# Single-pass matrix products whose moving operand is read as two interleaved halves: a spectral and attention mix on one core

## The chip, the cores and the metric

The kernel runs on one NeuronCore of one Trainium2 chip. The metric is the device time of one execution in microseconds. Three runs of the kernel before gave 1774.73, 1778.48 and 1774.53; their median is 1774.73.

TensorE (PE in the profile) multiplies: a weight load (PEld) puts the stationary operand into the array, and a matmul streams the moving operand's columns past it and adds into a bank of PSUM. VectorE (DVE), ScalarE (ACT) and GpSimd (POOL) work element by element, and SyncE (SP) starts most of the DMA transfers.

## What is computed

```python
a = jnp.einsum("bsd,ed->bse", x, dft_hid_re)
b = jnp.einsum("bsd,ed->bse", x, dft_hid_im)
y = jnp.einsum("ts,bse->bte", dft_seq_re, a) - jnp.einsum("ts,bse->bte", dft_seq_im, b)
...
q = (lambda x, *d: x.transpose(*d))((x @ wq).reshape(B, S, H, Dh), 0, 2, 1, 3)
k = x @ wk
v = x @ wv
scores = jnp.einsum("bhqd,bkd->bhqk", q, k) * (Dh ** -0.5)
p = _softmax(scores, axis=-1)
o = jnp.einsum("bhqk,bkd->bhqd", p, v)
return (lambda x, *d: x.transpose(*d))(o, 0, 2, 1, 3).reshape(B, S, H * Dh) @ wo
...
g = _sigmoid((x * gate_w).sum(-1, keepdims=True))
return g * a + (1 - g) * b
```

The sizes are S = 2048, D = 640, 32 heads of 20 with one key and one value head for all of them, everything in float32. In the last line a is the spectral branch's y and b is the attention branch.

## The kernel before, in words

**Number formats.** A value is split in two parts of the format float32r, a high part (the value rounded, made by a copy) and a low part (the value minus the high part). A product is then two or three matmuls of float32r operands: high by high, high by low, low by high. Both formats have four bytes to an element. A float32r matmul streams its columns once; the text calls it a single-pass product. One product, the attention weights by the values (`av`), has plain float32 operands instead, and its matmul streams the columns in two passes, as its time shows.

**Stages.** The work goes through five stages, each with its own products.

1. From 7 us: q and kv. `q_mm` (through `mm3`, L112) and `kv_mm` (L207) multiply x^T, split, by the weights; the moving operand is 512 columns of x^T. `q_out` and `kv_out` split the results and send them to DRAM and to the key tile `ks`. In the same stage the two hidden DFT matrices are loaded in ten pieces (`load_w`) and split (`split_w`).
2. From 89 us: `ab`, x by the hidden DFT matrices (`mm3_rows`, L120). The contraction of 128 rows is cut into two halves of 64 rows. Each half has its own rows of the array and its own bank, and the two run side by side. The moving operand is 320 columns of the split DFT matrix. Among these products stand the first 160 `a` units.
3. From 250 us to 1579 us: the main stage, in which four kinds of product are mixed. `a` (`a_unit`) is queries by keys, with 512 key columns moving; DVE reads each result of 128 x 512 and reduces it to a row maximum. `b` (`b_unit`) is keys by queries, with 512 query columns moving; ACT reads each result and takes the exponential into a tile `pt`. `av` (`av_mm`) multiplies `vsb` by four `pt` tiles of 512 columns, in four column groups of the array side by side. `y` (`Halves.run`) is the sequence DFT matrix by the results of `ab`, with 320 columns moving, 64 rows at a time; seven products replace eight. `a`, `b` and `y` each use one half of the array's rows, so that a product of one kind can run in the upper half beside another in the lower half. `av` uses all rows.
4. From 1579 us to 1702 us: the rest of `b`, `av` and `y`.
5. To the end: `o` (`o_group`, through `mm3`), the attention result by `wo`, with 320 columns of the split `wo` moving. `load_wo` splits `wo` in stage 4.

**What sets the order.** All engines but SP follow the order in which the code issues the instructions. In the main stage this order is the string PLAN: `V` is four `av` products, `0` and `1` are a `y` product in the lower or upper half of the rows, and a letter is an `a` or `b` unit with its half and one of six PSUM banks, which `a` and `b` share. A unit that takes a bank waits until DVE or ACT has read that bank's previous result.

Of the kernel before, what the change touches and what calls it, by code (L numbers as in the profile page):

```python
# [8 lines left out]
F32 = mybir.dt.float32  # L9
# [25 lines left out]
def kernel(  # L35
# [63 lines left out]

    nc.scalar.activation(gate, ident[:, :NT], AF.Exp)  # L100

    def words(ap):
        return ap.bitcast(F32) if ap.dtype == F32R else ap

# [6 lines left out]

    def mm3(ps, wh, wl, xh, xl, n, i):  # L112

        nc.tensor.matmul(ps, wh, xh, start=(i == 0), stop=False)  # L114
        nc.tensor.matmul(ps, wh, xl, start=False, stop=False)  # L115
        nc.tensor.matmul(ps, wl, xh, start=False, stop=(i == n - 1))  # L116

# [2 lines left out]
    def mm3_rows(ps2, wh, wl, xh, xl, n, i):  # L122
        for k, (w, x) in enumerate(((wh, xh), (wh, xl), (wl, xh))):
            for ps, r in zip(ps2, RG):
                nc.tensor.matmul(  # L125
                    ps, w[r], x[r], start=(i == 0 and k == 0), stop=(i == n - 1 and k == 2)
                )

    xT_v = xT.rearrange("(c p) t -> p c t", p=P)
# [13 lines left out]
    def split_w(i, c):  # L143
        if i < 2:
            if c == 0:
                wh.append(w2.tile([P, KC, D], F32R, name=f"wh{i}"))
                wl.append(w2.tile([P, KC, D], F32R, name=f"wl{i}"))
            split(wraw.pop((i, c)), wh[i][:, c], wl[i][:, c])

    xraw, xspl = {}, {}  # L150

# [13 lines left out]
    with ExitStack() as c1:  # L165
# [33 lines left out]
        def q_out(ps, n, m):  # L199
            ms, ts = slice(m * P, (m + 1) * P), slice(n * ROW, (n + 1) * ROW)  # L200
            qh = x1.tile([P, ROW], F32R, name="qh", bufs=4)
            ql = x1.tile([P, ROW], F32R, name="ql", bufs=4)
            nc.scalar.activation(qh, ps, AF.Copy)
            nc.vector.tensor_tensor(ql, ps, qh.bitcast(F32), op=ALU.subtract)
            move(qh_d[ms, ts], qh)
            move(ql_d[ms, ts], ql)

        def kv_mm(ps, n, c):
            xh, xl = xsp[n]
            nc.tensor.matmul(ps, kvgs[:, c], xh[:, c], start=(c == 0), stop=False)  # L210
            nc.tensor.matmul(ps, kvgs[:, c], xl[:, c], start=False, stop=(c == KC - 1))  # L211

        def kv_out(ps, n):
            ts = slice(n * ROW, (n + 1) * ROW)
            kvT = x1.tile([41, ROW], F32, name="kvT")
            kh = x1.tile([DH, ROW], F32R, name="kh")
            kl = x1.tile([DH, ROW], F32R, name="kl")
            nc.scalar.activation(kvT, ps[64:105], AF.Copy)
            nc.vector.tensor_tensor(kvT, ps[:41], kvT, op=ALU.add)
            nc.scalar.activation(kh, kvT[:DH], AF.Copy)  # L220
            nc.vector.tensor_tensor(kl, kvT[:DH], kh.bitcast(F32), op=ALU.subtract)
            for r0 in (0, 64):
                move(ks[r0 : r0 + 20, ts], kh)
                move(ks[r0 + 20 : r0 + 40, ts], kl)
                move(ks[r0 + 40 : r0 + 60, ts], kh)
            return kvT
# [95 lines left out]
    def a_unit(u, hh, tag="A"):  # L322

        p, r = divmod(u, 64)
        qb, c = divmod(r, 4)
        if r == 0 and p not in mx:
            mx[p] = sml.tile([P, 2, NT, 4], F32, name="mx")
        b = 64 * hh
        ps = bank(tag, f"a_{u}_{hh}")
        nc.tensor.matmul(  # L330
            ps,
            qs[p][b : b + 60, qb * P : (qb + 1) * P],
            ks[b : b + 60, c * ROW : (c + 1) * ROW],
            start=True,
            stop=True,
        )
        return nc.vector.tensor_reduce(mx[p][:, hh, qb, c : c + 1], ps, axis=AX.X, op=ALU.max)  # L337
# [223 lines left out]
    def load_wo(cs):  # L561
        for c in cs:
            raw = xp.tile([P, D], F32, tag=f"xr{c % 2}", name="woraw")
            move(raw, wo[c * P : (c + 1) * P])
            t = abp.tile([P, 2, D], F32R, tag=f"ab{c}0", name=f"wo{c}")
            split_w = (t[:, 0], t[:, 1])
            nc.vector.tensor_copy(split_w[0], raw)
            nc.vector.tensor_tensor(split_w[1], raw, split_w[0].bitcast(F32), op=ALU.subtract)
            wos[c] = split_w

    oT_v = oT_d.rearrange("(c p) t -> p c t", p=P)
# [64 lines left out]
    class Halves:  # L636
# [11 lines left out]
        def run(self, g):  # L648
# [4 lines left out]
            k = 0 if one else g  # L653
            start, stop = grp[k] == 0, grp[k] == (6 if one else 3) * NT - 1
            grp[k] += 1
            mm = nc.tensor.matmul(ps[g % len(ps)], w, x, start=start, stop=stop)  # L656
            if one:

                if not start and self.last != g:
# [122 lines left out]
    def b_unit(p, hh, kc, qc, tag):  # L782
        b = 64 * hh
        ps = bank(tag, f"b_{p}_{kc}_{qc}_{hh}")
        nc.tensor.matmul(  # L785
            ps,
            ks[b : b + 62, kc * P : (kc + 1) * P],
            qs[p][b : b + 62, qc * ROW : (qc + 1) * ROW],
            start=True,
            stop=True,  # L790
        )
        n = taken["b"][0] + taken["b"][1]
        slot = pick(waits(tag, n))
        t = pp.tile([P, ROW], F32, tag=f"pt{slot}", name="pt")
        halves.scored(nc.scalar.activation(t, ps, AF.Exp, scale=SCALE), n)  # L795
        pt[(hh, kc, qc)] = t, (n, slot)
# [293 lines left out]
```

## Time and profile before

| | |
|---|---|
| median of three runs | 1774.73 us (1774.53 to 1778.48) |
| the profiled execution, first to last instruction | 1773.9 us |
| mean granted TensorE clock | 1.000 |
| busy: PE, PEld, DVE, ACT, POOL | 1766.9, 1263.5, 1425.3, 1187.5, 819.7 us |
| DMA, share of the 16 engines | 42.4% in the largest queue |

The profiled execution is 0.8 us shorter than the median of the runs, so a difference in the profile can be set against the runs as it stands. PE's busy time is a union of pipelined instructions whose ends are modelled: a matmul of 320 columns is shown as 309 ns long, although the next one starts after 147 ns. How fast PE really streams is therefore read from the distance between starts.

### The profile page before, as it was taken

The numbers are of one execution on the slowest core, as the hardware profiler recorded it, in microseconds if no ns is written. First come the engines' busy times: TensorE is split into PE (matmuls) and PEld (weight loads), VectorE is DVE, ScalarE is ACT, GpSimd is POOL, SyncE is SP. The second block draws the span as 40 slices with busy tenths as digits, with TensorE's granted clock in tenths as the row PEclk, the third lists the DMA queues.
The fourth block names the chain that finished last, engine by engine and source line by source line (L and its number), as shares of the span: only waits on it lengthen the run. The fifth ranks groups of instructions, "written<-read, shape, count | busy, mean of one in ns | idle before, by whom it ended". The sixth has DMA issues, their size and how long they took to land.

```text
span 1773.9 us, 40730 instructions
## 1 busy us (share of the span) xinstructions
PE 1766.9 (100%) x16342; PEld 1263.5 (71%) x16342; DVE 1425.3 (80%) x2335; ACT 1187.5 (67%) x2327; POOL 819.7 (46%) x559
## 2 busy tenths in 40 slices
PE   9999999999999999999999999999999999999999
PEld 7799986666666666666666666666666666667789
DVE  4469999888888888888888888888888898855344
ACT  4432247777777777777777777777777777777731
POOL 1001227444455465656666565565654454442242
PEclk9999999999999999999999999999999999999999
DMA  8762324333334442534444444343443232325676
GB/s 268 233 198 95 116 98 133 108 130 100 125 106 146 119 132 92 174 99 159 151 143 123 156 131 132 103 148 106 142 141 113 86 119 89 103 67 188 191 230 206
DMA packets 131001, 243.87 MB, mean 137 GB/s; under 512 B 26356, under 2 KB 77556, under 8 KB 128292
## 3 DMA queue, kind: packets, MB, share of 16 engines
q1 hardware_dynamic: 130012, 238.00, 42.4%
q0 software_dynamic: 800, 3.28, 0.6%
q8 instruction: 128, 2.10, 0.5%
q14 instruction: 61, 0.50, 0.1%
HBM read 194.62 MB, written 50.86 MB: 138 GB/s over the span
## 4 chain that ended last, share of the span: by engine, by line
PE 99%; DMA 0%; ACT 0%; DVE 0%; issue 0%
PE av L799 27%; PE y L656 21%; PE b L785 17%; PE a L330 17%; PE ab L125 8%; PE q L114 1%; PE o L114 1%; PE q L116 1%; PE q L115 1%; PE o L116 1%; PE o L115 1%; PE kv L210 0%; PE kv L211 0%; DMA xr<-in_xT_dram 0%; ACT pt L795 0%; DVE mx L337 0%
## 5 line engine op out<-in xcount | busy, mean ns | idle before, releaser
L337 DVE TENSOR_REDUCE mx<-a 128x1 f32<-128x512 f32 x2048 | 1264.9, 683 | 170.5 <-PE a L330 111.3
L795 ACT ACTIVATE pt<-b 128x512 f32<-128x512 f32 x2048 | 1052.0, 618 | 327.8 <-PE b L785 193.5
L656 PE MATMUL y<-x,ch 64*128 64x320 f32 x3584 | 758.3, 309 | 0.9 <-ACT yt L685 0.9
L330 PE MATMUL a<-ks,qs 60*128 60x512 f32 x2048 | 736.4, 422 | 0.2 <-DVE mx L337 0.2
L785 PE MATMUL b<-qs,ks 62*128 62x512 f32 x2048 | 705.9, 421 | 0.3 <-ACT half L533 0.3
L656 PEld LDWEIGHTS y<-x,ch 64*128 64x128 f32 x3584 | 560.3, 185 | 23.0 <-issue 10.4
L656 PE MATMUL y<-x,cl 64*128 64x320 f32 x1792 | 514.9, 308 | 0.0
L799 PE MATMUL av<-pt,vsb 128*32 128x512 f32 x4096 | 502.9, 600 | 0.0
L330 PEld LDWEIGHTS a<-ks,qs 60*128 60x128 f32 x2048 | 350.1, 184 | 128.1 <-DVE mx L337 98.3
L785 PEld LDWEIGHTS b<-qs,ks 62*128 62x128 f32 x2048 | 340.3, 184 | 129.6 <-ACT pt L795 70.8
L459 POOL TENSOR_TENSOR craw<-craw 128x1024 f32<-128x1024 f32 x80 | 191.2, 2390 | 261.6 <-DMA craw<-in_cre_dram 115.4
L656 PEld LDWEIGHTS y<-x,cl 64*128 64x128 f32 x1792 | 308.4, 184 | 3.9 <-issue 2.5
L799 PEld LDWEIGHTS av<-pt,vsb 128*32 128x32 f32 x4096 | 106.6, 108 | 201.0 <-issue 179.0
L464 POOL TENSOR_TENSOR cl<-craw,ch 128x1024 fp32r<-128x1024 f32 x98 | 234.6, 2394 | 7.8
L463 POOL CAST ch<-craw 128x1024 fp32r<-128x1024 f32 x98 | 101.7, 1038 | 146.8 <-PE y L656 123.4
L125 PE MATMUL ab<-wh,xh 64*128 64x320 f32 x640 | 129.6, 307 | 0.0
L125 PE MATMUL ab<-wl,xh 64*128 64x320 f32 x640 | 129.3, 306 | 0.0
L125 PE MATMUL ab<-wh,xl 64*128 64x320 f32 x640 | 129.1, 305 | 0.0
L712 POOL TENSOR_TENSOR ya<-yt,ya 128x320 f32<-128x320 f32 x64 | 57.9, 920 | 102.5 <-ACT yt L685 101.8
L533 ACT ACTIVATE half<-ab 128x320 f32<-128x320 f32 x64 | 28.0, 438 | 114.8 <-PE ab L125 82.4
L125 PEld LDWEIGHTS ab<-wl,xh 64*128 64x128 f32 x640 | 91.5, 185 | 0.0
L125 PEld LDWEIGHTS ab<-wh,xl 64*128 64x128 f32 x640 | 91.3, 184 | 0.0
(88 smaller groups left out, 1082.7 us busy)
## 6 DMA issues: line engine op xcount, KB each, us to landing
craw<-in_cre_dram SPq DMA_DIRECT2D x96, 512.0 KB
craw<-in_cim_dram SPq DMA_DIRECT2D x96, 512.0 KB
xr<-x_d SPq DMA_DIRECT2D x88, 320.0 KB
qs<-qh_d SPq DMA_DIRECT2D x64, 160.0 KB
x_d<-both SPq DMA_DIRECT2D x64, 160.0 KB
ya<-y_d SPq DMA_DIRECT2D x64, 160.0 KB
y_d<-ya SPq DMA_DIRECT2D x64, 160.0 KB
xr<-in_xT_dram SPq DMA_DIRECT2D x20, 256.0 KB
```

What stands on the lines that cost most here:

```text
L114: nc.tensor.matmul(ps, wh, xh, start=(i == 0), stop=False)
L125: nc.tensor.matmul(ps, w[r], x[r], start=(i == 0 and k == 0), stop=(i == n - 1 and k == 2))
L330: nc.tensor.matmul(ps, qs[p][b : b + 60, qb * P : (qb + 1) * P], ks[b : b + 60, c * ROW : (c + 1) * ROW], start=True, stop=True,)
L337: return nc.vector.tensor_reduce(mx[p][:, hh, qb, c : c + 1], ps, axis=AX.X, op=ALU.max)
L459: eng.tensor_tensor(raw, raw, raws[1], op=PRODUCTS[n][0][1])
L463: eng.tensor_copy(h, raw)
L464: eng.tensor_tensor(l, raw, h.bitcast(F32), op=ALU.subtract)
L656: mm = nc.tensor.matmul(ps[g % len(ps)], w, x, start=start, stop=stop)
L712: nc.gpsimd.tensor_tensor(ya, yt, ya, op=how)
L785: nc.tensor.matmul(ps, ks[b : b + 62, kc * P : (kc + 1) * P], qs[p][b : b + 62, qc * ROW : (qc + 1) * ROW], start=True, stop=True,)
L795: halves.scored(nc.scalar.activation(t, ps, AF.Exp, scale=SCALE), n)
L799: nc.tensor.matmul(ps[32 * g : 32 * g + 32, :], vsb[:, kc, :], t, start=first, stop=last)
```

## The change

Every float32r matmul gets its moving operand through `woven`, which reads column 0, then the first column of the second half, then column 1, and so on: with 512 columns 0, 256, 1, 257, ..., with 320 columns 0, 160, 1, 161, .... The columns of the result stand in the order in which they were read. `av` is left as it was, and the weight loads are too.

So that the output comes out in its natural order, the order is undone where elements are copied anyway: at q's split and the DFT matrix's split by reading every fourth element and writing four runs (two woven products follow one another there), at kv's eviction and `wo`'s split by reading every second element and writing two runs. The splits of the DFT matrices and of `wo` are done in two halves of 320 columns each, since each half of 320 is a moving operand of its own.

```diff
+    def woven(ap):
+        return ap.rearrange("p (a b) -> p b a", a=2)
+    def runs(ap):
+        return ap.rearrange("p (a b) -> p a b", a=4)
+    def every(ap, n=4):
+        return ap.rearrange("p (b a) -> p a b", a=n)
...
     def mm3(ps, wh, wl, xh, xl, n, i):
-        nc.tensor.matmul(ps, wh, xh, start=(i == 0), stop=False)
-        nc.tensor.matmul(ps, wh, xl, start=False, stop=False)
-        nc.tensor.matmul(ps, wl, xh, start=False, stop=(i == n - 1))
+        nc.tensor.matmul(ps, wh, woven(xh), start=(i == 0), stop=False)
+        nc.tensor.matmul(ps, wh, woven(xl), start=False, stop=False)
+        nc.tensor.matmul(ps, wl, woven(xh), start=False, stop=(i == n - 1))
...
-                    ps, w[r], x[r], start=(i == 0 and k == 0), stop=(i == n - 1 and k == 2)
+                    ps, w[r], woven(x[r]), start=(i == 0 and k == 0), stop=(i == n - 1 and k == 2)
...
-            split(wraw.pop((i, c)), wh[i][:, c], wl[i][:, c])
+            raw = wraw.pop((i, c))
+            for e in range(2):
+                es = slice(e * HALF, (e + 1) * HALF)
+                hi, lo = wh[i][:, c, es], wl[i][:, c, es]
+                nc.scalar.activation(runs(hi), every(raw[:, es]), AF.Copy)
+                nc.vector.tensor_tensor(
+                    runs(lo), every(raw[:, es]), runs(hi).bitcast(F32), op=ALU.subtract
+                )
...
-            nc.scalar.activation(qh, ps, AF.Copy)
-            nc.vector.tensor_tensor(ql, ps, qh.bitcast(F32), op=ALU.subtract)
+            nc.scalar.activation(runs(qh), every(ps), AF.Copy)
+            nc.vector.tensor_tensor(runs(ql), every(ps), runs(qh).bitcast(F32), op=ALU.subtract)
...
-            nc.scalar.activation(kvT, ps[64:105], AF.Copy)
-            nc.vector.tensor_tensor(kvT, ps[:41], kvT, op=ALU.add)
+            kvW = kvT.rearrange("p (a b) -> p a b", a=2)
+            nc.scalar.activation(kvW, every(ps[64:105], 2), AF.Copy)
+            nc.vector.tensor_tensor(kvW, every(ps[:41], 2), kvW, op=ALU.add)
...
-            ks[b : b + 60, c * ROW : (c + 1) * ROW],
+            woven(ks[b : b + 60, c * ROW : (c + 1) * ROW]),
...
-            nc.vector.tensor_copy(split_w[0], raw)
-            nc.vector.tensor_tensor(split_w[1], raw, split_w[0].bitcast(F32), op=ALU.subtract)
+            for e in range(2):
+                es = slice(e * HALF, (e + 1) * HALF)
+                hi, lo = [w[:, es].rearrange("p (a b) -> p a b", a=2) for w in split_w]
+                nc.vector.tensor_copy(hi, every(raw[:, es], 2))
+                nc.vector.tensor_tensor(lo, every(raw[:, es], 2), hi.bitcast(F32), op=ALU.subtract)
...
-            mm = nc.tensor.matmul(ps[g % len(ps)], w, x, start=start, stop=stop)
+            mm = nc.tensor.matmul(ps[g % len(ps)], w, woven(x), start=start, stop=stop)
...
-            qs[p][b : b + 62, qc * ROW : (qc + 1) * ROW],
+            woven(qs[p][b : b + 62, qc * ROW : (qc + 1) * ROW]),
```

In `kv_mm` the two matmuls get `woven(xh[:, c])` and `woven(xl[:, c])` in the same way.

The order of the instructions on PE, POOL and SP is the same as before; on ACT and DVE the pieces of the DFT matrix split, and on DVE those of the `wo` split, become two. This is DVE in stage 1, between two results of q (`xl` is the low part of the next x, `ql` that of a q result, `wl` that of a DFT matrix piece), before:

```order
L204 TENSOR_TENSOR ql<-q_0_347,qh 128x512
L110 TENSOR_TENSOR wl_374<-wraw,wh_373 128x640
L110 TENSOR_TENSOR xl<-xr,xh 128x512
L204 TENSOR_TENSOR ql<-q_1_379,qh 128x512
L110 TENSOR_TENSOR wl_374<-wraw,wh_373 128x640
```

and in the changed kernel:

```order
L223 TENSOR_TENSOR ql<-q_0_347,qh 128x512
L165 TENSOR_TENSOR wl_374<-wraw,wh_373 128x320 x2
L122 TENSOR_TENSOR xl<-xr,xh 128x512
L223 TENSOR_TENSOR ql<-q_1_381,qh 128x512
L165 TENSOR_TENSOR wl_374<-wraw,wh_373 128x320 x2
```

Nothing has moved; one instruction of 640 columns is two of 320. On ACT the same piece reads, before:

```order
L203 ACTIVATE qh<-q_0_347 128x512
L109 ACTIVATE wh_373<-wraw 128x640
L109 ACTIVATE xh<-xr 128x512
L203 ACTIVATE qh<-q_1_379 128x512
L109 ACTIVATE wh_373<-wraw 128x640
```

and in the changed kernel:

```order
L222 ACTIVATE qh<-q_0_347 128x512
L164 ACTIVATE wh_373<-wraw 128x320 x2
L121 ACTIVATE xh<-xr 128x512
L222 ACTIVATE qh<-q_1_381 128x512
L164 ACTIVATE wh_373<-wraw 128x320 x2
```

The high part's copy is halved too, at the same place.

More of the change, by code (lines that the diff above doesn't have):

```diff
@@ L209, in kv_mm @@
             xh, xl = xsp[n]
-            nc.tensor.matmul(ps, kvgs[:, c], xh[:, c], start=(c == 0), stop=False)
-            nc.tensor.matmul(ps, kvgs[:, c], xl[:, c], start=False, stop=(c == KC - 1))
+            nc.tensor.matmul(ps, kvgs[:, c], woven(xh[:, c]), start=(c == 0), stop=False)
+            nc.tensor.matmul(ps, kvgs[:, c], woven(xl[:, c]), start=False, stop=(c == KC - 1))
         def kv_out(ps, n):
```

## The prediction

> **What bounds the kernel now.** I read the chain of waits first, then the stages, then the starts of single matmuls.
>
> ```profile
> PE 99%; DMA 0%; ACT 0%; DVE 0%; issue 0%
> PE av L799 27%; PE y L656 21%; PE b L785 17%; PE a L330 17%; PE ab L125 8%; PE q L114 1%; PE o L114 1%; PE q L116 1%; PE q L115 1%; PE o L116 1%; PE o L115 1%; PE kv L210 0%; PE kv L211 0%; DMA xr<-in_xT_dram 0%; ACT pt L795 0%; DVE mx L337 0%
> ```
>
> The end is set by TensorE from first to last. All of the chain but `av` (27%) is single-pass products, which are what the change touches. Next, engines by stage (columns: PE, PEld, DVE, ACT, POOL busy, clock, DMA share, GB/s); the stages are q and kv, `ab`, main, tail, `o`:
>
> ```profile
> 7.40:89.40 82.00, 82.00 (x352) 65.03 (x351) 41.98 (x65) 36.82 (x64) 4.29 (x8) 1.00 0.79 253
> 89.40:249.60 160.20, 160.20 (x2087) 160.06 (x2086) 138.98 (x245) 43.81 (x97) 24.80 (x21) 1.00 0.41 125
> 249.60:1579.00 1329.40, 1328.92 (x12106) 876.78 (x12103) 1166.31 (x1932) 1002.50 (x1971) 728.34 (x478) 1.00 0.40 124
> 1579.00:1702.00 123.00, 122.07 (x1320) 88.65 (x1318) 46.65 (x50) 88.59 (x176) 41.59 (x36) 1.00 0.54 172
> 1702.00:1773.90 71.90, 68.53 (x469) 68.20 (x465) 29.98 (x44) 12.02 (x15) 16.05 (x6) 1.00 0.65 210
> ```
>
> In the main stage DVE stands idle for only 163 of 1329 us, so a faster PE soon meets DVE there; in the other stages DVE and ACT have room. The clock is fully granted throughout.
>
> PE's busy time hides how fast it streams, so I take distances between starts. The timeline of PE alone, in the q stage, the `o` stage, and around two runs of `av`:
>
> ```profile
> 39.36 0.39 PE L114 MATMUL q<-xh,wqh 128*128 128x512 f32 x1
> ...
> 44.02 0.39 PE L116 MATMUL q<-xh,wql 128*128 128x512 f32 x1
> ...
> 1719.47 0.31 PE L115 MATMUL o<-wo,osp 128*128 128x320 f32 x1
> ...
> 1723.58 0.31 PE L116 MATMUL o<-wo,osp 128*128 128x320 f32 x1
> ...
> 901.25 1.06 PE L799 MATMUL av<-pt,vsb 128*32 128x512 f32 x8
> 902.25 0.49 PE L785 MATMUL b<-qs,ks 62*128 62x512 f32 x1
> ...
> 905.00 0.50 PE L330 MATMUL a<-ks,qs 60*128 60x512 f32 x1
> ...
> 907.60 0.50 PE L330 MATMUL a<-ks,qs 60*128 60x512 f32 x1
> ...
> 908.07 1.92 PE L799 MATMUL av<-pt,vsb 128*32 128x512 f32 x16
> 909.93 0.50 PE L785 MATMUL b<-qs,ks 62*128 62x512 f32 x1
> ```
>
> From the first q row to the last are 20 steps in 4.66 us: **0.233 us per product of 512 columns**. From the first `o` row to the last are 28 steps in 4.11 us: **0.147 us per 320 columns**. The 8 `av` matmuls (two groups of four, side by side) hold PE for 1.00 us until the next start, the 16 from 908.07 for 1.86 us: two more groups cost 0.86 us, so **0.430 us per group**, which streams 512 columns in two passes.
>
> The slope of the single-pass products is (0.233 - 0.147)/192 = 0.448 ns per column, with 0.0037 us per product besides. Two-pass, with the same fixed part: (0.430 - 0.0037)/1024 = 0.416 ns per column and pass. So a float32r stream runs 0.032 ns per column (7%) slower than the array runs `av` at the same clock. This loss grows with the columns, though each product loads 128 weight columns in both cases: it belongs to the moving stream and not to the weight load. In `av` a pass does not lose it. What the two differ in is how fast a stream asks for new four-byte elements.
>
> **The rate, part by part.** The change leaves the count and order of the PE instructions and alters only how the moving elements are fetched: from two places in turn, each advancing at half the pace. No row shows such a read on PE, so it is bounded from both sides. Best: the loss vanishes, 512 columns in 0.0037 + 512 x 0.416 = 0.217 us (16 ns less), 320 in 0.137 (10 ns less); without the fixed part, against two-pass pure, 18 and 13 ns. Worst: each turn to the other place throws away what a fetch had brought; then I count at least two fetches where there was one, and the nearest row of a stream at half pace is `av`'s, 0.430 for 512. I take the best case, because the one stream in the trace whose demand from a place is halved is also the one without the loss.
>
> By the Trainium skill ("TensorE: Matmul & The Clock Gate", Back-to-back issue gap) isolated warm matmuls are N/2.4 + 2.5 ns apart, 216 and 136 ns here; `av` agrees and the single-pass products do not, and the sum by it would be 17 and 11 ns per product instead of 16 and 10.
>
> How many products, in streams (two half-row products side by side are one):
>
> ```profile
> L114 PE MATMUL q<-xh,wqh 128*128 128x512 f32 x100 | 40.4, 404 | 0.0
> L210 PE MATMUL kv<-xh,kvgs 128*128 128x512 f32 x20 | 8.3, 416 | 0.8 <-DVE kvgs L110 0.8
> L125 PE MATMUL ab<-wh,xh 64*128 64x320 f32 x640 | 129.6, 307 | 0.0
> L114 PE MATMUL o<-wo,osp 128*128 128x320 f32 x120 | 37.1, 309 | 0.0
> L114 PE MATMUL o<-wo,qs 128*128 128x320 f32 x40 | 12.6, 314 | 0.0
> L656 PE MATMUL y<-x,ch 64*128 64x320 f32 x3041 | 690.0, 309 | 0.0
> L330 PE MATMUL a<-ks,qs 60*128 60x512 f32 x1889 | 673.7, 424 | 0.2 <-DVE mx L337 0.2
> L785 PE MATMUL b<-qs,ks 62*128 62x512 f32 x1896 | 671.7, 422 | 0.3 <-ACT half L533 0.3
> L656 PE MATMUL y<-x,cl 64*128 64x320 f32 x1520 | 469.2, 309 | 0.0
> ```
>
> The last four rows are the main stage alone. q has three such lines, kv two, `ab` three, `o` three of each kind.
>
> - q and kv: 340 x 0.233 = 79 us of the 82. Saved 340 x 16 ns = 5.4; I take 5, since the first products wait for DMA.
> - `ab`: 960 pairs x 0.147 = 141, and 160 `a` in 80 pairs x 0.233 = 19: 160 of 160.2 us, no wait at all. Saved 9.6 + 1.3; 10.5 taken, for its DVE is at 139 of 160 us.
> - `o`: 480 x 0.147 = 71 of 72 us. Saved 4.8; 5 taken.
>
> The tail, from the groups of that window:
>
> ```profile
> L656 PE MATMUL y<-x,ch 64*128 64x320 f32 x543 | 68.3, 307 | 0.9 <-ACT yt L685 0.9
> L656 PE MATMUL y<-x,cl 64*128 64x320 f32 x272 | 45.7, 306 | 0.0
> L785 PE MATMUL b<-qs,ks 62*128 62x512 f32 x154 | 34.8, 409 | 0.0
> ```
>
> 407 pairs of `y` x 10 ns and 77 pairs of `b` x 16 ns: 5.3; 5 taken.
>
> - Main: 2280 pairs of `y` x 10 ns = 22.8, 1892 pairs of `a` and `b` x 16 ns = 30.3: **53 us at most**. How much of it arrives depends on DVE:
>
> ```profile
> 905.57 3.77 DVE L337 TENSOR_REDUCE mx<-a 128x1 f32<-128x512 f32 x6 [0.27 <-PE a L330]
> 910.50 1.89 DVE L337 TENSOR_REDUCE mx<-a 128x1 f32<-128x512 f32 x3 [1.16 <-PE a L330]
> DVE mx L337 <- PE a L330: 104.5, 163, 2.4
> DVE mx L337 <- PE b L785: 55.0, 86, 1.8
> ```
>
> Between two `av` runs the `a` products start at 905.00, four times between, and at 907.60: 0.52 us apart. DVE reads one in 3.77/6 = 0.63. It falls behind inside the block, and in the next `av` run catches up and stands idle (1.16 us). The six banks end this: where a block has filled them, `a` and `b` start when a bank is read, and 16 ns saved on a product come back as wait. Only blocks that reach `av` without such a wait pass the saving on; there DVE enters the `av` run with more unread results and idles less. Its 249 pauses of 0.64 us on average (the two wait rows, main stage alone) are what can shrink. Lower end 0 (all blocks wait), upper end 53; I find no side that the rows favour and take half, **26 us**. A loss is excluded: the order is the same and no unit starts later than before.
>
> **The splits.** The strided copies cost DVE and ACT time off the path:
>
> ```profile
> L109 ACT ACTIVATE wh<-wraw 128x640 fp32r<-128x640 f32 x10 | 7.4, 736 | 6.8 <-DMA wraw<-in_wrT_dram 6.1 <-DMA wraw<-in_wiT_dram 0.6
> L110 DVE TENSOR_TENSOR wl<-wraw,wh 128x640 fp32r<-128x640 f32 x10 | 8.2, 818 | 6.6 <-ACT wh L109 6.5
> L203 ACT ACTIVATE qh<-q 128x512 fp32r<-128x512 f32 x20 | 11.6, 598 | 24.8 <-PE q L116 13.6 <-DMA qh_d<-qh 5.4 <-issue 3.5
> L204 DVE TENSOR_TENSOR ql<-q,qh 128x512 fp32r<-128x512 f32 x20 | 13.5, 686 | 22.2 <-ACT qh L203 16.7 <-DMA ql_d<-ql 5.5
> ```
>
> If a half of 320 cost as much as a whole of 640 and q's strided reads twice what they do now, stage 1 would get 7.4 + 11.6 = 19 us on ACT and 8.2 + 13.5 = 22 on DVE; they are busy 37 and 42 of its 82 us, and q's eight banks give each result several products' time to be read. Below, they cost nothing more than now. `wo`'s five pieces lie in the tail, with DVE busy 47 of 123 us. I cost all of it at nothing; if the cover is gone, the most is a q result late for its bank, some 1 to 2 us at the end of the stage.
>
> **Sum:** 5 + 10.5 + 26 + 5 + 5 = 51.5. The profiled execution spans 1773.9, 0.8 us less than the median of the runs: 1774.7 - 51.5 = **1723 us**.
>
> **The rivals.**
>
> *All of it arrives* (0.08): waits for banks stay as they are. 5.4 + 10.9 + 53 + 5.3 + 4.8 = 79, so 1695; with 18 and 13 ns, 2388 x 18 + 4128 x 13 = 97, so 1678. For it: every stage but main is PE alone. Against it: the 0.52 against 0.63 above.
>
> *The rate returns, or half returns, and main gains nothing* (0.13): 25.5 or less from the other stages, 1749 to 1762.
>
> *The pace is a limit per element* (0.10): a float32r element cannot be fetched faster than one in 0.448 ns from wherever it lies, and two places change nothing. For it: `av`, whose pass runs without loss, may fetch an element once for both passes, which relieves a limit per element too. Then nothing moves: 1775, within 2 us.
>
> *A fetch is wasted at every turn* (0.16, slower): the path that brings moving elements keeps one place at a time, so that a fetch which served neighbours serves one column. It decides as soon as a product's distance rises above 0.233 or 0.147 us. At two fetches for one all streams double: 2388 x 0.233 + 4128 x 0.147 = 1163 us more, 2938. For it: nothing in the trace reads the moving operand in any other way than end to end. Against it: a reader that needs several fetches in flight to keep 0.448 ns per column has room for two places. The Trainium skill ("Advanced Engine Details and Errata", SBUF Cachelines) speaks for this rival: full performance needs following accesses to hit the same 16-byte line, at least twice. A woven stream changes the line at every column. By that page four columns share a line, and a lost line each time would be up to four times the streams, an estimate of 5260 us; no run here shows it yet.
>
> **How the numbers follow.** The forecast, 1723, has 0.53, with its own range 1702 to 1748 (main from 47 us down to 0). About 0.3% (5 us) is what a measurement of this kernel can tell from no change. Faster: 0.53 + 0.08 + 0.13 = 0.74; same 0.10; slower 0.16. The range reaches from 1688 to 1780, over the neutral case; it leaves out the wasted fetch and the best corner.
>
> **What would show it.** Right: starts 0.217 us apart in q and 0.137 in `o`; `ab` 10 us shorter; the main stage some 26 us shorter, with DVE's pauses down from 163 us by about as much; `av` groups unchanged. Wrong in the rate: the distances stay at 0.233 and 0.147, or rise. Wrong in the main stage: the `o` and `ab` stages shrink as said, and main by nothing or by 50 us. Wrong in the splits: the first stage does not shrink and PE waits there for ACT or DVE on a q bank.

## The result and the profile after

The changed kernel takes **1747.2 us** (median of 4 runs, 1746.5 to 1749.1) against 1775.1 for the kernel before in the same comparison: a ratio of 0.984, with a 95% interval of 0.983 to 0.986. The forecast was 1723, with a range of 1688 to 1780. The direction is right, and the saving, 28 us, is a little over half of the 51.5 forecast. The profiled execution spans 1745.2 us.

The chain of waits of the changed kernel, by engine and by line:

```profile
PE 94%; DMA 3%; DVE 1%; ACT 1%; SPq 1%; issue 0%; POOL 0%; DVEq 0%; POOLq 0%; ACTq 0%
PE av L822 28%; PE y L679 21%; PE b L808 17%; PE a L350 17%; PE ab L137 7%; PE q L126 1%; PE q L127 1%; PE q L128 1%; DMA oraw<-rx_d 1%; PE o L128 1%; PE o L126 1%; SPq L118 1%; PE o L127 1%; DVE mx L357 0%; DMA ql_d<-ql 0%
```

TensorE is still nearly all of it, but other engines now appear. The timeline of PE in the changed kernel, in q and in `o`:

```profile
29.82 0.38 PE L127 MATMUL q<-xl,wqh 128*128 128x512 f32 x1
...
35.00 0.38 PE L127 MATMUL q<-xl,wqh 128*128 128x512 f32 x1
...
1699.71 0.30 PE L126 MATMUL o<-wo,osp 128*128 128x320 f32 x1
...
1703.92 0.30 PE L127 MATMUL o<-wo,osp 128*128 128x320 f32 x1
```

24 steps in 5.18 us are 0.216 us per product of 512 columns (0.233 before); 31 steps in 4.21 us are 0.136 per 320 columns (0.147 before). A product saves 17 and 11 ns, and the loss of the float32r stream against `av` is gone. Next, the busy time of the engines by stage, in the columns used before:

```profile
7.10:92.40 85.30, 80.78 (x352) 67.52 (x350) 51.47 (x75) 48.07 (x74) 4.29 (x8) 0.96 0.78 241
92.40:241.90 149.50, 148.78 (x2086) 148.54 (x2086) 135.73 (x245) 43.69 (x97) 24.97 (x21) 1.00 0.44 135
241.90:1558.90 1317.00, 1316.32 (x12106) 849.64 (x12104) 1164.15 (x1931) 1000.99 (x1971) 722.57 (x478) 1.00 0.40 126
1558.90:1672.70 113.80, 112.73 (x1293) 81.73 (x1290) 46.26 (x59) 86.05 (x176) 37.94 (x33) 1.00 0.53 173
1672.70:1745.20 72.50, 68.12 (x500) 65.74 (x496) 32.77 (x46) 12.53 (x16) 20.35 (x9) 1.00 0.71 228
```

Cut in both traces at the same events (first kv, first `ab`, first `y`, end of the last `a`, first `o`, end), in us; the first line above starts one microsecond later, at the first q, and the prediction cut tail and `o` at 1702 us:

| stage | before | after | difference | forecast |
|---|---|---|---|---|
| q and kv | 83.0 | 86.4 | +3.4 | -5 |
| `ab` | 160.0 | 149.5 | -10.5 | -10.5 |
| main | 1329.2 | 1317.0 | -12.2 | -26 |
| tail | 119.2 | 113.8 | -5.4 | -5 |
| `o` | 76.1 | 72.5 | -3.6 | -5 |

Two stages miss: the first gets longer, and the main stage gives less than half of what was expected of it.

**The first stage.** The groups of ACT and DVE in the changed kernel's first stage show which of the copies got dear:

```profile
L164 ACT ACTIVATE wh<-wraw 128x320 fp32r<-128x320 f32 x20 | 18.7, 986 | 6.7 <-DMA wraw<-in_wrT_dram 4.6 <-DMA wraw<-in_wiT_dram 2.1
L222 ACT ACTIVATE qh<-q 128x512 fp32r<-128x512 f32 x20 | 11.6, 597 | 18.5 <-PE q L128 7.9 <-DMA qh_d<-qh 5.4 <-issue 4.8
L165 DVE TENSOR_TENSOR wl<-wraw,wh 128x320 fp32r<-128x320 f32 x20 | 18.4, 950 | 6.1 <-ACT wh L164 6.1
```

q's eviction, which reads PSUM with a step of four, takes what it took (597 ns, 598 before). The DFT matrix split, which reads SBUF with a step of four elements, takes 986 ns on average for 320 columns (754 to 1073) where 736 ns did for 640: 1.97 us for a piece instead of 0.74 on ACT, and 1.90 instead of 0.82 on DVE. The timelines of POOL, ACT and PE at one place of the stage show what follows from it:

```profile
47.91 0.54 POOL L118 DMA_DIRECT2D wraw<-in_wrT_dram  x1 [3.48 <-DVE wl L165]
...
50.53 1.44 ACT L164 ACTIVATE wh<-wraw 128x320 fp32r<-128x320 f32 x2 [2.79 <-DMA wraw<-in_wrT_dram]
51.88 0.61 ACT L121 ACTIVATE xh<-xr 128x512 fp32r<-128x512 f32 x1
...
48.27 0.48 PE L230 MATMUL kv<-xl,kvgs 128*128 128x512 f32 x1 [0.48 <-DVE xl L122]
52.55 0.80 PE L229 MATMUL kv<-xh,kvgs 128*128 128x512 f32 x1 [3.79 <-ACT xh L121]
...
55.70 0.63 PE L128 MATMUL q<-xh,wql 128*128 128x512 f32 x1
56.13 0.63 PE L126 MATMUL q<-xh,wqh 128*128 128x512 f32 x1
```

A piece is loaded into one of two buffers, so its load waits until DVE has split the piece before the last (3.48 us). ACT waits for the load (2.79 us). Behind that split, in ACT's order, stands the high part of the next x, and kv waits for that (3.79 us): the next start comes 4.28 us after the last. After the pause the products of q run 0.43 us apart instead of 0.216 until 58.7 us, as the last two rows show. The granted clock there is 0.50:

```profile
56.00:58.00 2.00, 2.00 (x6) 1.55 (x6) 1.30 (x3) 1.15 (x2) 0.46 (x1) 0.50 0.81 246
```

Over the whole stage it is 0.96, where the kernel before had 1.00.

**The main stage.** DVE's pauses there, of the changed kernel, from the view of one tile (us, times):

```profile
  PE a L350: 96.2, 158
  PE b L808: 48.0, 83
  PE y L679: 7.7, 12
```

They sum to 151.9 us, against 162.1 before. DVE's work is nearly the same (1164 us busy against 1166), so 10 of the 12 us that the main stage saved are pauses of DVE that got shorter.

### The profile page after: what moved, and what is told of

Same layout as the page of the kernel before. It is cut to its first block, busy times and chain, and to the rows that moved or that the text cites. A ratio compares the mean times of both kernels' runs of the same rounds, so it can differ in the third digit from the quotient of the medians.

```text
span 1745.2 us, 40761 instructions
## 1 busy us (share of the span) xinstructions
PE 1732.0 (99%) x16342; PEld 1217.9 (70%) x16342; DVE 1432.1 (82%) x2355; ACT 1194.6 (68%) x2337; POOL 814.8 (47%) x559
## 4 chain that ended last, share of the span: by engine, by line
PE 94%; DMA 3%; DVE 1%; ACT 1%; SPq 1%; issue 0%; POOL 0%; DVEq 0%; POOLq 0%; ACTq 0%
PE av L822 28%; PE y L679 21%; PE b L808 17%; PE a L350 17%; PE ab L137 7%; PE q L126 1%; PE q L127 1%; PE q L128 1%; DMA oraw<-rx_d 1%; PE o L128 1%; PE o L126 1%; SPq L118 1%; PE o L127 1%; DVE mx L357 0%; DMA ql_d<-ql 0%
## 5 line engine op out<-in xcount | busy, mean ns | idle before, releaser
L679 PE MATMUL y<-x,ch 64*128 64x320 f32 x3584 | 728.4, 304 | 1.1 <-ACT yt L708 1.1
L350 PE MATMUL a<-ks,qs 60*128 60x512 f32 x2048 | 722.2, 414 | 0.3 <-DVE mx L357 0.2
L808 PE MATMUL b<-qs,ks 62*128 62x512 f32 x2048 | 695.1, 414 | 0.3 <-ACT half L553 0.3
L679 PEld LDWEIGHTS y<-x,ch 64*128 64x128 f32 x3584 | 549.9, 186 | 21.6 <-issue 10.5
L679 PE MATMUL y<-x,cl 64*128 64x320 f32 x1792 | 507.8, 304 | 0.0
L350 PEld LDWEIGHTS a<-ks,qs 60*128 60x128 f32 x2048 | 350.5, 184 | 140.0 <-DVE mx L357 102.1
L137 PEld LDWEIGHTS ab<-wh,xl 64*128 64x128 f32 x640 | 97.5, 185 | 0.0
L137 PEld LDWEIGHTS ab<-wl,xh 64*128 64x128 f32 x640 | 97.5, 186 | 0.0
```

The costliest lines, as they stand in the source:

```text
L137: nc.tensor.matmul(ps, w[r], woven(x[r]), start=(i == 0 and k == 0), stop=(i == n - 1 and k == 2))
L350: nc.tensor.matmul(ps, qs[p][b : b + 60, qb * P : (qb + 1) * P], woven(ks[b : b + 60, c * ROW : (c + 1) * ROW]), start=True, stop=True,)
L679: mm = nc.tensor.matmul(ps[g % len(ps)], w, woven(x), start=start, stop=stop)
L808: nc.tensor.matmul(ps, ks[b : b + 62, kc * P : (kc + 1) * P], woven(qs[p][b : b + 62, qc * ROW : (qc + 1) * ROW]), start=True, stop=True,)
```

## The experiments

The theory after the result: the stream's rate is what the forecast says, and all that is missing was taken in two places, by the strided SBUF reads of the DFT matrix split and by waits for the six banks of the main stage. The first two kernels below were run four times, the others once; runs of the kernel before differ by up to 4 us among themselves.

### The DFT matrices split as before

```diff
-            raw = wraw.pop((i, c))
-            for e in range(2):
-                ...
-                nc.scalar.activation(runs(hi), every(raw[:, es]), AF.Copy)
-                nc.vector.tensor_tensor(runs(lo), every(raw[:, es]), runs(hi).bitcast(F32), op=ALU.subtract)
+            split(wraw.pop((i, c)), wh[i][:, c], wl[i][:, c])
```

> The changed kernel with one edit: the DFT matrices are split as before the change, contiguously in ten pieces of 640 columns, so that the output's columns come out in another order; all matmuls are woven as in the changed kernel. Theory: stage 1 lost its gain to the SBUF reads of every fourth element (986 ns for 320 columns on ACT where 640 contiguous ones took 736), which made the x split and with it kv late. Then stage 1 falls from 85.6 us to about 77 and the time from 1747 to about 1738.5. Rival: q's and kv's strided evictions from PSUM, which stay in this run, or the shorter products themselves outrunning the loads, hold PE up; then stage 1 stays near 85 us and the time near 1747.

Measured: 1737.7 us, a ratio of 0.979 (0.977 to 0.980) to the kernel before. The first stage of this run, and its main stage:

```profile
6.20:82.80 76.60, 76.13 (x353) 64.79 (x353) 41.72 (x65) 37.42 (x65) 4.29 (x8) 1.00 0.85 274
233.00:1549.90 1316.90, 1316.23 (x12106) 849.62 (x12103) 1163.85 (x1931) 1001.04 (x1971) 722.51 (x478) 1.00 0.39 126
```

The stage falls from 86.4 to 76.6 us, 6.4 below the kernel before, and the clock is whole again, as the theory had it. q's and kv's strided evictions were still in, so they are not the cause. Set side by side, product by product, the changed kernel is 1.5 us behind this run after its first 12 products, long before the first split at 37.5 us, and still 1.7 us behind just before the pause; it is 6.5 us behind after the pause, 9.2 at the end of the half clock and 9.6 at the end of the stage. So nearly 8 us are the split's, and the first 1.5 are not.

The edit takes back three things at once: the read with a step of four, the writes in four runs, and two instructions in place of one. q's eviction writes four runs too and takes no longer for it. On `wo`, where a piece is halved as well but the step is two, two halves take DVE 0.18 to 0.19 us more than a whole, against 1.08 us more for a piece of the DFT matrices. That leaves the read with a step of four as the main cost; it was not run alone.

### The order undone at evictions: a better version

```diff
+                two = [t.rearrange("p (a b) -> p a b", a=2) for t in (half, both)]
-                nc.scalar.activation(half, ps[0], AF.Copy, scale=sg)
-                nc.vector.scalar_tensor_tensor(both, ps[1], sg, half, op0=ALU.mult, op1=ALU.add)
+                nc.scalar.activation(two[0], every(ps[0], 2), AF.Copy, scale=sg)
+                nc.vector.scalar_tensor_tensor(
+                    two[1], every(ps[1], 2), sg, two[0], op0=ALU.mult, op1=ALU.add
+                )
...
-        nc.scalar.activation(grp["t"][k], ps[k], AF.Copy)
+        nc.scalar.activation(grp["t"][k].rearrange("p (a b) -> p a b", a=2), every(ps[k], 2), AF.Copy)
```

The split of the DFT matrices is the contiguous one, as in the run above.

> As the run before, but with the output in its natural order again: the order is undone at the eviction of ab (ACT's and DVE's reads of PSUM, every second element, written as two runs) and at the eviction of y, instead of at the split of the DFT matrices. Theory: reads of PSUM with a step cost nothing (q's eviction took 597 ns with a step of four and 598 without), so 1738 to 1740 us, and the evictions keep 437, 486 and 455 ns. Rival: steps cost on PSUM reads as they do on SBUF reads, once two engines read at once; then the 128 evictions of ab and 64 of y get about twice as long, DVE in the ab stage goes over the stage's 150 us, and the time is 1755 or more.

Measured: **1736.65 us**, a ratio of 0.978 (0.976 to 0.979) to the kernel before; the interval lies wholly below that of the changed kernel (0.983 to 0.986). The groups of the evictions that now read PSUM with a step of two:

```profile
L548 DVE SCALAR_TENSOR_TENSOR both<-ab,half 128x320 f32<-128x320 f32 x64 | 30.8, 483 | 11.1 <-ACT half L547 8.0 <-DMA x_d<-both 3.0
L547 ACT ACTIVATE half<-ab 128x320 f32<-128x320 f32 x64 | 28.0, 437 | 104.6 <-PE ab L137 99.2 <-PE a L343 5.2
L704 ACT ACTIVATE yt<-y 128x320 f32<-128x320 f32 x56 | 26.3, 470 | 0.6 <-PE a L343 0.6
```

483, 437 and 470 ns, against 486, 438 and 455 before: a step on the PSUM side cost nothing, or 15 ns, and the rival fell. The time is 1 to 3 us below what was expected. This version beats both kernels with the output in its order.

### Both readers of the main stage halved, without and with woven products

```diff
-        return nc.vector.tensor_reduce(mx[p][:, hh, qb, c : c + 1], ps, axis=AX.X, op=ALU.max)
+        return nc.vector.tensor_reduce(mx[p][:, hh, qb, c : c + 1], ps[:, :256], axis=AX.X, op=ALU.max)
...
-        halves.scored(nc.scalar.activation(t, ps, AF.Exp, scale=SCALE), n)
+        halves.scored(nc.scalar.activation(t[:, :256], ps[:, :256], AF.Exp, scale=SCALE), n)
```

Here `t` is one of 16 tiles that stay, whose second half is set once.

> The kernel before the change, with its two readers in the main stage halved: DVE reduces 256 of the 512 score columns and ACT takes the exponential of 256 of 512 (the other half of each pt tile is set once to 1), so the row maxima and the attention weights cover half of the scores; every matmul is as before. Theory (banks held by DVE and ACT take the gain): without waits for banks the main stage is shorter than 1329 us already here, by 10 to 50 us, and it is the base for the next run. Rival (PE's own streams and their changes between products set the main stage): it stays within 5 us of 1329.

> The changed kernel with the contiguous DFT split (output columns in another order) and the same halved readers as the run before (half of the scores reduced, half of the exponentials taken). Theory: with no waits for banks, the woven streams save in the main stage nearly what they can, 45 to 53 us against the run before, instead of the 12.5 between the two original kernels. Rival: the mixed streams of the main stage do not get faster than the 12.5 us show; then the difference in the main stage stays between 8 and 20 us.

Measured: 1757.8 and 1671.9 us. The main stage of the first, and of the second:

```profile
250.00:1560.80 1310.80, 1306.83 (x12104) 862.45 (x12101) 741.72 (x1948) 687.55 (x1971) 728.44 (x478) 1.00 0.39 126
```

```profile
232.40:1485.80 1253.40, 1249.34 (x12105) 816.48 (x12103) 734.02 (x1948) 681.61 (x1971) 721.94 (x478) 1.00 0.41 132
```

With DVE and ACT reading half as much, weaving saves 57.4 us in the main stage, not 12, a little more than the 45 to 53 expected. Over the whole kernel it saves 85.8 us. The full saving by the measured distances is 1892 x 17 ns + 2280 x 11 ns = 57 us in the main stage and 2388 x 17 ns + 4128 x 11 ns = 86 us in all: the whole of it arrives once the readers keep up. Slower streams in the mixed stage are not what the halving cures: in the changed kernel as it stands, `y` products of this stage start at 1002.86, 1003.00, 1003.13 and 1003.27, 0.137 us apart. The kernel before gains only 18 us in this stage from the halved readers.

Even then PE does not run at its bare rate. At the measured distances the products of the main stage, side by side, take 2280 x 0.147 + 1892 x 0.233 + 940 groups of `av` x 0.430 = 1180 us before and 1123 us woven. Both halved runs lie 130 us above that. This rest does not change with weaving; what it is made of was not tested.

### One reader halved

```diff
-        return nc.vector.tensor_reduce(mx[p][:, hh, qb, c : c + 1], ps, axis=AX.X, op=ALU.max)
+        return nc.vector.tensor_reduce(mx[p][:, hh, qb, c : c + 1], ps[:, :256], axis=AX.X, op=ALU.max)
```

in the one run, and the other run has the edit of the exponential alone; both with woven products.

> All matmuls woven, DFT split contiguous (output columns in another order), and DVE alone halved: it reduces 256 of the 512 score columns, so the row maxima cover half of the scores; ACT takes all exponentials. Base without halving: main stage 1317 us; with both halved: 1253. Theory (DVE is the reader that holds the banks, as the prediction argued): main stage near 1265, most of the 63 us. Rival (DVE and ACT hold them about equally, since a and b share the six banks): near 1290 or above, and the same for ACT alone.

> As the run before, but ACT alone halved: the exponential of 256 of 512 columns (the other half of each pt tile is set once to 1), DVE reduces all columns. Theory (DVE holds the banks): main stage above 1305. Rival (both about equally): near 1290. If both single halvings leave the main stage above 1300, either reader alone is enough to hold it.

The main stage with DVE halved, and with ACT halved:

```profile
234.30:1539.90 1305.60, 1305.26 (x12105) 839.03 (x12102) 735.91 (x1932) 997.54 (x1971) 723.12 (x478) 1.00 0.39 127
```

```profile
232.60:1546.20 1313.60, 1308.47 (x12107) 839.47 (x12103) 1166.83 (x1947) 690.39 (x1971) 721.85 (x478) 1.00 0.39 126
```

The runs took 1726.6 and 1731.9 us. The main stage's 1316.9 falls by 11.3 with DVE relieved, by 3.3 with ACT relieved, and by 63.5 with both. Neither reader alone is the one that holds; either one is enough. The expectation that DVE holds the banks fell with the first run: 1305.6, far from 1265. The second run's "above 1305" came true all the same, as did "near 1290 or above" of the first rival, and the last sentence of the second expectation is what happened.

Why either is enough follows from the code: `a` and `b` share the banks, and PE issues in order. The waits agree. A unit's weight load comes ahead of its matmul, and in the main stage of the changed kernel the loads of `a` wait for DVE 102.1 us in 146 waits, those of `b` for ACT 69.3 us in 89. With DVE halved, and with ACT halved, they are (us, times, longest):

```profile
PEld b L801 <- ACT pt L811: 75.9, 118, 0.8
PEld a L343 <- DVE mx L350: 60.4, 72, 0.8
```

```profile
PEld a L343 <- DVE mx L350: 114.0, 185, 4.5
PEld b L804 <- ACT pt L814: 38.6, 46, 0.8
```

The waits for the relieved reader fall to half in number and by two fifths in time, and those for the other one grow. They are not the lost time itself, since part of each lies under a product that still streams.

### Only some products woven

```diff
-            ks[b : b + 60, c * ROW : (c + 1) * ROW],
+            woven(ks[b : b + 60, c * ROW : (c + 1) * ROW]),
...
-            qs[p][b : b + 62, qc * ROW : (qc + 1) * ROW],
+            woven(qs[p][b : b + 62, qc * ROW : (qc + 1) * ROW]),
```

in the first run, and in the second only

```diff
-            mm = nc.tensor.matmul(ps[g % len(ps)], w, x, start=start, stop=stop)
+            mm = nc.tensor.matmul(ps[g % len(ps)], w, woven(x), start=start, stop=stop)
```

> The kernel before the change with only the a and b products woven (the key and query columns are left in that order, so the attention result is permuted); y, ab, q, kv, o and all copies as before. Theory: in a block one half of the array's rows runs scores and the other y, and the in-order issue ties them; 16 ns less per score pair is mostly taken by waits for banks: main stage 2 to 8 us shorter, other stages unchanged, 1767 to 1773. Rival (each product's saving counts by itself): 1892 x 16 ns = 30 us shorter at most, and 12.5 x 30/53 = 7 us if what was lost is lost in proportion.

> The kernel before the change with only the y products woven (y's columns are left in that order); a, b, ab, q, kv, o and all copies as before. Theory: y is not what waits for banks, but the scores beside it set the pace in most blocks: main stage 3 to 8 us shorter, tail 4 us shorter, 1763 to 1768. Rival (y sets the pace, scores have slack): 20 us or more of the 23 arrive in main, 1748 to 1752.

Measured: 1760.9 and 1769.3 us. The main stage of the first, and of the second:

```profile
247.00:1565.30 1318.30, 1317.86 (x12105) 876.73 (x12102) 1164.23 (x1931) 1001.52 (x1971) 727.67 (x478) 1.00 0.40 125
```

```profile
247.60:1576.50 1328.90, 1328.24 (x12107) 849.72 (x12104) 1166.05 (x1931) 1001.81 (x1971) 727.09 (x478) 1.00 0.40 125
```

Woven scores alone bring 10.9 us in the main stage, more than the 2 to 8 expected; woven `y` alone brings 0.3 there, less than the 3 to 8 expected, and 4 in the tail, as expected. Of the 12.2 us, nearly all is the scores'. As the main stage stands, a shorter `y` shortens nothing. With both readers halved it does: the 57.4 us saved there are more than the scores' 1892 x 17 ns = 32 us. (Both runs are single profiles, and their first stage, which has no edit, differs from the kernel before by about 1 us.)

### Other orders of reading

Three kernels with other orders, one per stage, on the kernel before. Its contiguous copies stay, so that the columns are permuted. The code is that of the first; the comments are not in it and name the orders of all three in turn.

```diff
+    def pat_q(ap):   # every fourth; then every second; then pairs from two halves
+        return ap.rearrange("p (b a) -> p a b", a=4)
+    def pat_ab(ap):  # four quarters in turn; then 0 4 1 5 2 6 3 7; then eight places in turn
+        return ap.rearrange("p (a b) -> p b a", a=4)
+    def pat_o(ap):   # every second; then every fourth; then 0 2 1 3
+        return ap.rearrange("p (b a) -> p a b", a=2)
...
-        nc.tensor.matmul(ps[32 * g : 32 * g + 32, :], vsb[:, kc, :], t, start=first, stop=last)
+        nc.tensor.matmul(ps[32 * g : 32 * g + 32, :], vsb[:, kc, :], t.rearrange("p (a b) -> p b a", a=2), start=first, stop=last)
```

The last change, `av` woven, is in the first kernel alone.

> The kernel before the change with other reading orders, one per stage, and all copies as before, so that columns are left permuted: q (512 columns) reads every fourth element (0, 4, 8, ..., then 1, 5, ...); ab (320) reads four interleaved quarters; o (320) reads every second element; av (two passes) reads two interleaved halves; kv, a, b and y as before. Read are the distances between starts. Theory A (a new four-byte element right behind the last one is what costs, any jump avoids it): q 0.216, ab 0.136, o 0.136, av unchanged at 0.430 per group. Theory B (two or more places in turn are needed, because each place then has time to fetch on): ab 0.136, o stays at 0.147, q at or above 0.233, av 0.430. Rival C (every fourth element costs as it did on ACT and DVE, where 320 took as long as 780 contiguous ones would): q about 0.5.

> The kernel before the change with other reading orders again, all copies as before and columns left permuted: q (512) reads every second element (0, 2, 4, ..., then 1, 3, ...); ab (320) interleaves within eight neighbours (0, 4, 1, 5, 2, 6, 3, 7, then 8, ...); o (320) reads every fourth element; the rest as before. Theory A (any jump helps): 0.216, 0.136, 0.136. Theory B (two places far apart in turn): q 0.233, ab 0.147, o 0.147 or more. If ab is 0.136, neighbouring fours in turn are enough, and the distance of the halves does not matter.

> The kernel before the change with a third set of reading orders, all copies as before and columns left permuted: q (512) reads pairs in turn from two halves (0, 1, 256, 257, 2, 3, ...); ab (320) reads eight interleaved places; o (320) reads 0, 2, 1, 3, then 4, 6, 5, 7. Theory (a fetch brings two neighbouring elements and takes about 0.89 ns, and two elements from one fetch right after one another leave no time for the next fetch, while turns between two fetches overlap them): q stays at 0.233, since both elements of a pair follow one another; o 0.136, since the two pairs of four are read in turn; ab 0.170 or more. Rival (a fetch brings four neighbours, one line of four): o stays at 0.147 and q changes to 0.22 to 0.23.

They took 2043.6, 1900.0 and 1924.4 us. The timeline of PE in the first of them: q (14 steps in 6.46 us), one half of `ab` (5 steps in 0.85), a run of 16 woven `av`, `o` (18 steps in 5.10):

```profile
59.47 0.64 PE L124 MATMUL q<-xh,wqh 128*128 128x512 f32 x1
...
65.93 0.64 PE L126 MATMUL q<-xh,wql 128*128 128x512 f32 x1
...
199.82 0.47 PE L135 MATMUL ab<-wh,xh 64*128 64x320 f32 x2
...
200.67 0.47 PE L135 MATMUL ab<-wh,xl 64*128 64x320 f32 x2
...
1002.75 2.38 PE L809 MATMUL av<-pt,vsb 128*32 128x512 f32 x16
1005.05 0.50 PE L340 MATMUL a<-ks,qs 60*128 60x512 f32 x1
...
1949.63 0.46 PE L126 MATMUL o<-wo,osp 128*128 128x320 f32 x1
...
1954.73 0.46 PE L126 MATMUL o<-wo,osp 128*128 128x320 f32 x1
```

The second: q (14 steps in 6.34), one half of `ab` (4 steps in 0.54), `o` (18 steps in 5.22):

```profile
59.38 0.63 PE L125 MATMUL q<-xl,wqh 128*128 128x512 f32 x1
...
65.72 0.63 PE L124 MATMUL q<-xh,wqh 128*128 128x512 f32 x1
...
200.10 0.30 PE L135 MATMUL ab<-wl,xh 64*128 64x320 f32 x1
...
200.64 0.30 PE L135 MATMUL ab<-wh,xl 64*128 64x320 f32 x1
...
1799.63 0.47 PE L124 MATMUL o<-wo,osp 128*128 128x320 f32 x1
...
1804.85 0.47 PE L124 MATMUL o<-wo,osp 128*128 128x320 f32 x1
```

The third: q (5 steps in 1.64), `ab` (4 steps in 1.09), `o` (29 steps in 4.26):

```profile
59.52 0.50 PE L124 MATMUL q<-xh,wqh 128*128 128x512 f32 x1
...
61.16 0.50 PE L126 MATMUL q<-xh,wql 128*128 128x512 f32 x1
...
199.76 0.60 PE L135 MATMUL ab<-wl,xh 64*128 64x320 f32 x2
...
200.85 0.60 PE L135 MATMUL ab<-wh,xl 64*128 64x320 f32 x2
...
1869.74 0.31 PE L124 MATMUL o<-wo,osp 128*128 128x320 f32 x1
...
1874.00 0.31 PE L126 MATMUL o<-wo,osp 128*128 128x320 f32 x1
```

| order of the moving elements | us per product | ns per column |
|---|---|---|
| two places in turn, halves apart | 0.216 (512), 0.136 (320) | 0.42 |
| 0 4 1 5 2 6 3 7 | 0.135 (320) | 0.42 |
| end to end | 0.233 (512), 0.147 (320) | 0.46 |
| 0 2 1 3 | 0.147 (320) | 0.46 |
| four places in turn | 0.170 (320) | 0.53 |
| pairs in turn from two halves | 0.328 (512) | 0.64 |
| eight places in turn | 0.273 (320) | 0.85 |
| every second element | 0.453 (512), 0.283 (320) | 0.88 |
| every fourth element | 0.461 (512), 0.290 (320) | 0.90 |

A jump as such does not help: every second and every fourth element cost twice the time of end to end, so Theory A fell. Theory B, two or more places in turn, is right for two only: four places took 0.170 us where it said 0.136, and every second element took 0.283 where it said 0.147. The places need not be far apart either: four neighbours in turn with the next four do as well as halves. Rival C, about 0.5 us for every fourth element, came near with 0.461. The theory that a fetch brings two elements fell with 0 2 1 3, which stays at the end-to-end time, and its rival with the pairs, which got slower than either said.

What the rows have in common is narrow: of these orders only a turn at every column between two groups of four neighbours beats end to end. Turns inside such a group (0 2 1 3) change nothing. Pairs taken in turn from two halves are slower, and so are four and eight places. Which part of the read path does this is left open. `av`, with its two passes, lost, where both theories had it unchanged: the run of 16 holds PE for 2.30 us where it held it for 1.86, 0.11 us more per group.

## Why the prediction was right, and where it was wrong

The direction and the range are right, the sum is not. 1747.2 lies at the far end of the forecast's own range (1702 to 1748; its terms give 1749), within 2 us of the rival in which main gains nothing (1749 to 1762). Two terms missed to the same side, main by 14 us and the first stage by 8, so that the number stayed inside that range is in part luck. The stages, one by one, tell which steps held.

- **The rate: right.** 0.216 and 0.136 us were measured, 0.217 and 0.137 forecast. The saving per product was put at 16 and 10 ns, and is 17 and 11, 79 us in sum against 86. The 0.430 us of an `av` group, from which it was worked out, come from rows that are rounded to 0.01 us, so a forecast that is 1 ns off is closer than its rows allowed.
- **Its reason: half right.** The argument was that a stream which asks each place for elements at half the pace loses nothing. Two places in turn do that. Four places ask each at a quarter of the pace and are slower (0.170 us), which that argument would not have given. And `av`, the row it leaned on, gets slower when woven. The experiments confirm the price, not the reason for it.
- **`ab`, tail: right**, 10.5 for 10.5 and 5.4 for 5. **`o`: nearly**, 3.6 for 5; one weight load waited 1.2 us for the late split of an attention result (`osp`), and in the contiguous-split run and the better version the stage takes 71.4 and 70.9 us, about 5 us less than before.

- **The main stage: right in kind, wrong in size.** That the readers of the banks take the rest of the saving is shown by the halved readers (12 against 57 us); that they do so through the six banks is read from the code and the waits. The term that was mis-sized is the share that arrives: a half was taken for want of a row that favoured a side, and 12.2 of 57 us is about a fifth. The step also said that it depends on DVE. It depends on DVE and ACT together, and relieving DVE alone gave 11 of 63 us.
- **The splits: wrong.** The failed step is "I cost all of it at nothing". The size was not far off: 11 us more on ACT and 10 on DVE, within the 19 and 22 that were allowed. What failed is the cover. Busy shares of the stage were compared, 37 and 42 of 82 us, where the split stands in ACT's order ahead of the x split that kv needs, and holds one of two buffers that the next load needs. The price was put at 1 to 2 us, for a q result late for its bank; PE waited for the x split instead, and then ran at half the clock. The stage came out 8.4 us above its forecast, and 9.8 us came back with the contiguous split, nearly 8 of them the split's. The doubling was also allowed for in the wrong place: q's reads with a step, from PSUM, cost nothing, and those of the DFT matrices, from SBUF, 2.7 times the time of a piece on ACT.
- **The rivals.** "A fetch is wasted at every turn" did not happen for two halves, but its price is what every second element costs: 0.453 us against 0.467, twice 0.233. "All of it arrives" is what the kernels with halved readers show, and not the kernel as it stands.

The Trainium skill ("Advanced Engine Details and Errata", SBUF Cachelines) gives full performance to following accesses in one 16-byte line and asks for two hits on a line. The group of four elements in the table is 16 bytes, which agrees. The rest does not, for PE's moving operand: turning to another line at every column is the fastest order here (0.136 us), staying in the line the next (0.147), and two hits on a line in a row, with a step of two, take 0.283. For ACT and DVE the page agrees with the step of four elements on SBUF (986 ns), and with the step of two on `wo` as far as it goes: 320 columns took DVE 331 and 510 ns, and 640 contiguous ones 485 and 826. Two halves are 177 and 194 ns more than a whole, which may be the fixed cost of a second instruction; no run here separates the two.

## What to carry to other kernels

In this kernel a float32r product whose moving operand is read as two places in turn, halves or neighbouring fours, took 7% less time than end to end; not with the other orders tried, and not in a two-pass float32 product. Undo the order where PSUM is read (597 against 598 ns with a step of four), not where SBUF is read with a step of four. And look for the readers of PE's banks before you count on a saving there: here all of it arrived with both readers halved, and a fifth in the main stage as it stands. For a copy that gets dearer, ask what stands behind it on its engine and who waits for its buffer, not how busy the engine is on average.

## What was not expected of the hardware

- Reading four places in turn is slower than end to end (0.170 against 0.147 us), though two places are faster (0.136).
- A step of two elements costs a float32r product nearly as much as a step of four (0.453 and 0.461 us for 512 columns).
- `av`, two-pass float32, loses 0.11 us of 0.430 per group when its moving operand is woven.
- After 3.79 us without a product, PE was granted half its clock (0.50) from 52 to 58 us, with the products 0.43 us apart.
